# The second layer's output products with the weights held still and turned afterwards, new durations in the planner, and an earlier due time for attention

## The chip, the cores and the metric

The kernel runs on one core of a Trainium2 chip. The metric is the device time of one execution in microseconds, as the median of several runs. The profile is of one such execution.

## The reference

Three stages, one after the other. The first is a linear attention with a decay per head, in chunks of time; its output is laid out as 3072 tokens of 256 features. Two dense layers follow, each with 2048 hidden units, the first with an ELU between its products and the second with a Mish.

```python
# attention, per chunk of 32 steps (batch 4, 8 heads, 768 steps, head_dim 32, d_state 16)
cum = np.cumsum(log_a, axis=-1)
L = np.exp(cum[:, :, :, None] - cum[:, :, None, :]) * causal
y = np.einsum('bhij,bhjd->bhid', (C @ B^T) * L, x) + np.einsum('bhin,bhnd->bhid', C, state) * np.exp(cum)
state = np.exp(sum(la)) * state + sum_j B_j x_j exp(cum_last - cum_j)

x = y.transpose(0, 2, 1, 3).reshape(3072, 256)
h = x @ w_in                     # first layer
x = np.where(h > 0, h, np.exp(np.minimum(h, 0)) - 1) @ w_out
h = x @ w_in2                    # second layer
out = (h * np.tanh(np.log1p(np.exp(h)))) @ w_out2
```

## The kernel before, in words

**Tiles and blocks.** Attention goes in 32 tiles of 96 steps, eight in time for each of the four batches. The two layers go in seven blocks of tokens, BL = 384, 384, 512, 512, 512, 512, 256. The list `order` alternates layers: (1,0), (1,1), (2,0), (2,1), (1,2), (1,3), (2,2), (1,4), (2,3), and so on to (2,6), where (2,3) is layer 2 of block 3. Each block has 16 slots, one for each 128 hidden units. A slot has an h part (`emit_h`, six products: two halves of the contraction by high x high, high x low and low x high parts of the split 32-bit numbers), then the activation and the split of its result into gh and gl, and an output part some five slots later (`LAG`).

**Output products.** In layer 1 (`emit_y1`) the weights are stationary and the tokens move: two accumulators of 128 features x all tokens of the block, three products each, so six of 512 columns in a large block. In layer 2 (`emit_y2`) the activations are stationary, 128 tokens at a time, and the weights move: for each 128 tokens one product of gh with high and low weights (512 columns) and one of gl with the high weights (256 columns). The accumulator holds 128 tokens x 512 values; ScalarE or VectorE scales its second half (`y2_out1`), VectorE adds the first (`y2_out2`), and one or two DMAs store rows of 256 numbers (`y2_store`).

**PSUM.** Eight banks: two for h (`ph`), two "acc", two "accb" (`pa`), two "s" (`px`) for attention. Layer 2 takes its first two accumulators from acc and the third and fourth from accb. Layer 1 takes two from acc, and its odd slots of h from f = 5 on (or from the start, if the block before is also layer 1) from accb; this is `h_other`.

**What sets the order.** Nothing is scheduled at run time. The program lists steps, each with the engines that can do it, a duration, the steps that it needs, and sometimes a due time `dl`. `run_steps` plays these through, always takes the step whose latest start (`late`, found backwards from due times) is earliest, and writes the instructions in that order on each engine's queue. Rings (`take`) stand for buffers. `alt` gives a step to one of two engines. The due time of an h slot is `slot_time`; attention steps inherit theirs through what they feed. `lock` holds the steps of VectorE that are kept apart from GpSimd's. Loads of ScalarE's function tables ("exp", "mish") are counted in.

**Attention, as far as it is touched.** For each tile: `three_parts` (splits of B and C on ScalarE and VectorE or GpSimd, then a DMA that transposes, stk to t), `at_diff` and `at_mask` and `at_exp` (the decays d), `at_scores` (TensorE, s), `at_p` (VectorE, r), `at_y` and `at_st` (TensorE, ys), and `at_y_hi` and `at_y_lo` (the split of the output into xyh and xyl, the first layer's input). The first eight tiles go without the DMA (`at_tr0`, `at_scores0`). All loads and all stores but one are issued on SP's queue, in order.

**Weights.** Each of 32 pieces (`jobs`: i1, o1, i2, o2) is loaded as raw bits and split by `job_1` to `job_5`; `job_4` writes the high part and `job_5` the low part.

Of the kernel before, what the change touches and what calls it, by code (L numbers as in the profile page):

```python
# [18 lines left out]
def tile_chain(  # L19
# [25 lines left out]
    FP = 2  # L45
    NP = NF // FP
# [59 lines left out]
    class Need:  # L106
# [10 lines left out]
        d=Ring(2), r=Ring(1), t=Ring(1), r1=Ring(1), bw=Ring(2), o=Ring(2), stk=Ring(1),  # L117
# [264 lines left out]
    def job_4(j, eng):  # L382
        key, k = jobs[j]
        z, n = divmod(j, NJ)
        wt[key, k] = wpool.tile([128, 2, 2, 256], F32R, tag=f"w{z + 1}_{n}", name=f"w{key}{k}")
        copy(eng, w_hi(key, k), raw[j][:, :, :, 1].bitcast(F32))

    def job_5(j, eng):
        key, k = jobs[j]
        w = raw.pop(j)[:, :, :, 1].bitcast(F32)  # L390
        alu(eng).tensor_tensor(out=w_lo(key, k), in0=w, in1=w_hi(key, k).bitcast(F32), op=ALU.subtract)
# [480 lines left out]

    def emit_y2(s, k):
        _, c, f = at_slot(s)
        n = min(128, BL[c] - 128 * k)
        if f == 0:

            acc[2, c, k] = pa.tile([128, 2, DM], F32, tag="acc" if k < 2 else "accb", name="acc")[0:n]
# [4 lines left out]
        nc.tensor.matmul(out=y, lhsT=gh[:, ts], rhs=w[:, :, f % FP, :], start=(f == 0), stop=False)  # L883
        nc.tensor.matmul(out=y[:, 0], lhsT=gl[:, ts], rhs=w[:, 0, f % FP, :], start=False, stop=(f == NF - 1))  # L884

    def y2_out1(c, k, eng):
        n = min(128, BL[c] - 128 * k)
        o = tl["o", c, k] = at.tile([128, DM], F32, tag="o", name="o", bufs=2)[0:n]
        if eng == V:
            nc.vector.tensor_scalar_mul(o, acc[2, c, k][:, 1], 1.0 / WS)  # L890
        else:
            nc.scalar.activation(out=o, in_=acc[2, c, k][:, 1], func=AF.Copy, scale=1.0 / WS)
# [62 lines left out]
    s_d6 = step((PE, 0.1, decays_6), s_d5, s_c2, an)  # L955
# [8 lines left out]
    for j, (key, k) in enumerate(jobs):  # L964
# [21 lines left out]
        rf.append(q5)  # L986
        w_ready[key, k] = [q4, q5]
# [21 lines left out]
    def out_of_y(i, y):  # L1009

        YHI[i], YLO[i] = {}, {}
        for q in pieces(i):
            w = q[3] / T
            YHI[i][q[0]] = step((A, 0.14 + 0.14 * w, lambda q=q: at_y_hi(i, *q)), y, xy_f["x", q[0]][1])
            YLO[i][q[0]] = step((V, 0.10 + 0.2 * w, lambda q=q: at_y_lo(i, *q)), YHI[i][q[0]])
        return list(YHI[i].values()) + list(YLO[i].values())

    def three_parts(i, need):
# [3 lines left out]
        a1 = step((A, 0.88, lambda: at_split_1(i)), need, sn)  # L1022
        a2 = step(alt(lambda e: at_split_2(i, e), (V, 0.50), (G, 0.50)), a1, rn)
        a3 = step((A, 0.68, lambda: at_split_3(i)), a2)
        a4 = step(alt(lambda e: at_split_4(i, e), (V, 0.50), (G, 0.50)), a3)
# [17 lines left out]
    for i in range(NB):  # L1043
        cold = i in TR0
        if cold:
            tf, tn = take("s")
            tr = step((PE, 0.64, lambda i=i: at_tr0(i)), s_lc[i], s_lb[i], s_c2, tn)
# [16 lines left out]
        else:  # L1064
# [50 lines left out]
    for i in range(NB, tiles):  # L1115
# [16 lines left out]
        for g in range(2):  # L1132
            f = lambda e, i=i, g=g: at_diff(i, g * H // 2, (g + 1) * H // 2, e)
            dd.append(step(alt(f, (G, 1.0), (V, 0.47)), lc, s_q6))
            lock.add(dd[-1])
        mk = step((G, 0.95, lambda i=i: at_mask(i)), dd)
        ex = step((A, 0.78, lambda i=i: at_exp(i)), mk)
        table[ex] = "exp"
        cs = step((G, 0.95, lambda i=i: at_cs(i)), l96, lc, s_d5)
        r_f, r_n = take("r")  # L1140
        rc = step((V, 0.56, lambda i=i: at_rc(i)), cs, r_n)
# [8 lines left out]
        if cold:  # L1150
            pz = []
            for z in range(2):
                two = [take("s"), take("s")]
                sc = step((PE, 0.65, lambda i=i, z=z: at_scores0(i, z)), a2, [n for _, n in two])
# [8 lines left out]
        if c + 1 < NCH:  # L1163
            y = step((PE, 0.65, lambda i=i: (at_y(i), at_st(i))), pz, rc, rc2, LX[i], pn, SO[i - NB], b1, b2)
# [11 lines left out]
    for s in range(len(order) * NF):  # L1176
# [3 lines left out]
        if f == 0 and s:  # L1180
            acc_f[blk] = [take("acc" if k < 2 else "accb") for k in range(2 if layer == 1 else NK[c])]
# [43 lines left out]
        if layer == 1:  # L1225
# [5 lines left out]
            if f == NF - 1:  # L1231
                EV[1, c] = []
                for k in range(2):
# [3 lines left out]
                    acc_f[blk][k][0].extend([p, q])  # L1237
        else:
# [45 lines left out]
```

## Time and profile before

| | us |
|---|---|
| median of 3 runs | 613.85 (613.49 to 615.1) |
| the profiled execution | 614.17 |
| its span, first to last instruction | 612.1 |
| around the span | 2.07 |
| TensorE busy | 598.7 (98% of the span) |
| VectorE busy | 433.2 (71%) |
| ScalarE busy | 377.4 (62%) |
| GpSimd busy | 177.6 (29%) |

In the profile the engines are PE (TensorE's products), PEld (its loads of weights), DVE (VectorE), ACT (ScalarE), POOL (GpSimd) and SP (the queue of DMAs). A row of a timeline has the start in us, the duration, engine, line of the kernel, instruction, what it writes and reads, and its shape. Products overlap, so the pace of a stream is the distance between starts, not the duration of one. In brackets stands how long the engine had been idle, and what ended that. A row of the view of stretches has, for each engine, busy us and in brackets the count of instructions.

### The profile page before, as it was taken

The numbers are of one execution on the slowest core, as the hardware profiler recorded it, in microseconds if no ns is written. First come the engines' busy times: TensorE is split into PE (matmuls) and PEld (weight loads), VectorE is DVE, ScalarE is ACT, GpSimd is POOL, SyncE is SP. The second block draws the span as 40 slices with busy tenths as digits, with TensorE's granted clock in tenths as the row PEclk, the third lists the DMA queues.
The fourth block names the chain that finished last, engine by engine and source line by source line (L and its number), as shares of the span: only waits on it lengthen the run. The fifth ranks groups of instructions, "written<-read, shape, count | busy, mean of one in ns | idle before, by whom it ended". The sixth has DMA issues, their size and how long they took to land.

```text
span 612.1 us, 10993 instructions
## 1 busy us (share of the span) xinstructions
PE 598.7 (98%) x3876; PEld 506.4 (83%) x3876; DVE 433.2 (71%) x948; ACT 377.4 (62%) x705; POOL 177.6 (29%) x238
## 2 busy tenths in 40 slices
PE   6899999999999999999999999999999999999997
PEld 5677799999987878888878888878888888988896
DVE  5899899987887888765877766767764545744454
ACT  4699999976878775554786644597544214542121
POOL 2346455222556545100544301536100000200000
PEclk9599999999999999999999999999999999999999
DMA  7799894205564543002463302533300000000010
GB/s 149 190 244 297 260 260 103 56 9 99 104 121 85 111 81 68 5 0 52 72 114 73 80 1 27 104 82 74 62 0 1 1 0 19 19 1 0 1 36 18
DMA packets 133655, 47.09 MB, mean 77 GB/s; under 512 B 116672, under 2 KB 122432, under 8 KB 133600
## 3 DMA queue, kind: packets, MB, share of 16 engines
q1 hardware_dynamic: 133488, 46.29, 34.5%
q8 instruction: 30, 0.49, 0.4%
q14 instruction: 25, 0.20, 0.1%
q10 hardware_dynamic: 112, 0.10, 0.0%
HBM read 32.31 MB, written 3.24 MB: 58 GB/s over the span
## 4 chain that ended last, share of the span: by engine, by line
PE 92%; DMA 3%; ACT 2%; DVE 1%; issue 1%; SPq 0%; ACTq 0%; DVEq 0%
PE h L789 15%; PE h L790 14%; PE h L791 14%; PE acc L883 14%; PE acc L884 7%; PE acc L852 6%; PE acc L853 6%; PE acc L854 6%; PE acc L857 4%; PE ys L716 2%; DMA t<-stk 2%; PE s L667 2%; PE s L679 1%; ACT L836 1%; PE ys L746 1%
## 5 line engine op out<-in xcount | busy, mean ns | idle before, releaser
L789 PE MATMUL h<-xyh,wi 128*128 128x512 f32 (+2 forms) x448 | 168.5, 376 | 1.0 <-ACT w L836 0.9
L790 PE MATMUL h<-xyl,wi 128*128 128x512 f32 (+2 forms) x448 | 162.2, 362 | 0.2 <-DVE xyl L733 0.2
L791 PE MATMUL h<-xyh,wi 128*128 128x512 f32 (+2 forms) x448 | 162.0, 362 | 0.0
L883 PE MATMUL acc<-wo,gh 128*128 128x512 f32 x384 | 142.5, 402 | 0.0
L832 DVE TENSOR_TENSOR gl<-w,gh 128x512 fp32r<-128x512 f32 (+2 forms) x181 | 122.5, 678 | 21.5 <-ACT gh L375 12.9
L836 ACT ACTIVATE w<-h 128x512 f32<-128x512 f32 (+2 forms) x112 | 59.4, 536 | 100.9 <-PE h L791 68.7
L884 PE MATMUL acc<-wo,gl 128*128 128x256 f32 x384 | 107.5, 280 | 0.0
L377 DVE CAST gh<-w 128x512 fp32r<-128x512 f32 (+2 forms) x114 | 47.0, 414 | 74.8 <-PE acc L883 51.2
L789 PEld LDWEIGHTS h<-xyh,wi 128*128 128x128 f32 x448 | 85.0, 190 | 17.4 <-ACT w L836 2.5
L791 PEld LDWEIGHTS h<-xyh,wi 128*128 128x128 f32 x448 | 85.0, 190 | 10.7
L790 PEld LDWEIGHTS h<-xyl,wi 128*128 128x128 f32 x448 | 85.2, 190 | 9.7 <-DVE xyl L733 0.5
L883 PEld LDWEIGHTS acc<-wo,gh 128*128 128x128 f32 x384 | 72.2, 188 | 15.5
L805 ACT ACTIVATE w<-h 128x512 f32<-128x512 f32 (+2 forms) x96 | 51.7, 540 | 51.1 <-PE h L791 37.1
L884 PEld LDWEIGHTS acc<-wo,gl 128*128 128x128 f32 x384 | 72.5, 189 | 2.2
L832 POOL TENSOR_TENSOR gl<-w,gh 128x512 fp32r<-128x512 f32 (+2 forms) x27 | 29.6, 1096 | 147.6 <-ACT gh L375 95.6
L375 ACT ACTIVATE gh<-w 128x512 fp32r<-128x512 f32 (+2 forms) x94 | 54.9, 584 | 27.8 <-PE acc L853 23.4
L852 PE MATMUL acc<-gh,wo 128*128 128x512 f32 (+2 forms) x192 | 70.2, 365 | 0.0
L854 PE MATMUL acc<-gl,wo 128*128 128x512 f32 (+2 forms) x192 | 69.6, 363 | 0.0
L853 PE MATMUL acc<-gh,wo 128*128 128x512 f32 (+2 forms) x192 | 69.6, 362 | 0.0
L813 DVE TENSOR_SCALAR w<-w 128x512 f32<-128x512 f32 (+2 forms) x74 | 30.5, 414 | 26.2 <-ACT w L805 25.2
L595 POOL TENSOR_TENSOR d<-bc,dk 32x384 f32<-32x384 f32 x28 | 27.9, 999 | 68.8 <-DVE gl L832 41.8
L821 DVE TENSOR_TENSOR w<-h,w 128x512 f32<-128x512 f32 (+2 forms) x74 | 46.6, 631 | 1.5
(102 smaller groups left out, 821.4 us busy)
## 6 DMA issues: line engine op xcount, KB each, us to landing
d<-cum_d SPq DMA_DIRECT2D x31, 288.0 KB, 3.9
raw<-in_moe_w_in_dram SPq DMA_DIRECT2D x16, 512.0 KB, 6.5
raw<-in_moe_w_out_dram SPq DMA_DIRECT2D x16, 512.0 KB, 5.9
xs<-in_x_dram SPq DMA_DIRECT2D x32, 96.0 KB, 2.9
bc<-in_C_dram SPq DMA_DIRECT2D x32, 48.0 KB, 2.4
bc<-in_B_dram SPq DMA_DIRECT2D x32, 48.0 KB, 2.7
out_dram<-o SPq DMA_DIRECT2D x15, 96.0 KB, 1.9
bc<-bc SPq DMA_DIRECT2D x84, 16.0 KB, 2.4
```

Of the source, the lines that this page charges most:

```text
L375: nc.scalar.activation(out=out, in_=in_, func=AF.Copy)
L789: nc.tensor.matmul(out=h, lhsT=hi[:, k, fs], rhs=xh[:, k, :], start=(k == 0), stop=False)
L790: nc.tensor.matmul(out=h, lhsT=hi[:, k, fs], rhs=xl[:, k, :], start=False, stop=False)
L791: nc.tensor.matmul(out=h, lhsT=lo[:, k, fs], rhs=xh[:, k, :], start=False, stop=(k == 1))
L805: nc.scalar.activation(out=new_w(s), in_=st[s][0], func=AF.Exp)
L832: alu(eng).tensor_tensor(out=gl, in0=w, in1=gh.bitcast(F32), op=ALU.subtract)
L836: nc.scalar.activation(out=new_w(s), in_=st[s][0], func=AF.Mish)
L852: nc.tensor.matmul(out=y, lhsT=hi[:, f % FP, ds], rhs=gh, start=(f == 0), stop=False)
L853: nc.tensor.matmul(out=y, lhsT=lo[:, f % FP, ds], rhs=gh, start=False, stop=False)
L854: nc.tensor.matmul(out=y, lhsT=hi[:, f % FP, ds], rhs=gl, start=False, stop=(f == NF - 1))
L883: nc.tensor.matmul(out=y, lhsT=gh[:, ts], rhs=w[:, :, f % FP, :], start=(f == 0), stop=False)
L884: nc.tensor.matmul(out=y[:, 0], lhsT=gl[:, ts], rhs=w[:, 0, f % FP, :], start=False, stop=(f == NF - 1))
```

## The change

- **Output products of layer 2** in blocks 0 to 5 (`emit_yt`): as in layer 1, the weights are stationary, and there are two accumulators of 128 x tokens, from acc. At the end of a block VectorE turns each accumulator in squares of 32 x 32 into SBUF (`yt_turn`), ScalarE or VectorE scales the whole in place (`yt_scale`), and one DMA for each 32 tokens stores it (`yt_store`), in pieces of 64 numbers. Block 6 keeps `emit_y2`, with its views changed to the new order of columns; its last addition is split in two.
- **Weights o2** are written by `job_4` and `job_5` with columns regrouped, so that the turned squares land in order (`by_rows`, `from_raw`).
- **Banks**: no accumulator takes accb any more. `h_other` puts every odd slot of h there, in both layers, but for block 6 of layer 2 and the first slots.
- **Planner**: durations of attention's steps are changed, most for TensorE and GpSimd.
- **Due time**: the split `at_y_lo` of tiles from 14 on gets one, 10 us (`EARLY`) before the first slot that reads it.

The diff, cut to its core:

```diff
+    EARLY = 10.0
...
+    def by_rows(key, w):
+        return w.rearrange("p k f (b q) -> p (f b) k q", q=32) if key == "o2" else w
+
+    def from_raw(key, r):
+        w = r[:, :, :, 1].bitcast(F32)
+        return w.rearrange("p f (b k q) -> p (f b) k q", k=2, q=32) if key == "o2" else w
...
-        copy(eng, w_hi(key, k), raw[j][:, :, :, 1].bitcast(F32))
+        copy(eng, by_rows(key, w_hi(key, k)), from_raw(key, raw[j]))
...
-        return layer == 1 and f % 2 and (f >= 5 or s >= NF and order[s // NF - 1][0] == 1)
+        return f % 2 and (f >= 5 or s >= NF and (c < NBL - 1 or layer == 1))
...
+    def emit_yt(s):
+
+        _, c, f = at_slot(s)
+        if f == 0:
+            acc[2, c] = [pa.tile([128, MT], F32, tag="acc", name="acc")[:, 0:BL[c]] for _ in range(2)]
+        _, _, gh, gl = st.pop(s)
+        hi, lo = [w("o2", f // FP)[:, :, f % FP] for w in (w_hi, w_lo)]
+        for k in range(2):
+            y = acc[2, c][k]
+            nc.tensor.matmul(out=y, lhsT=hi[:, k], rhs=gh, start=(f == 0), stop=False)
+            nc.tensor.matmul(out=y, lhsT=lo[:, k], rhs=gh, start=False, stop=False)
+            nc.tensor.matmul(out=y, lhsT=hi[:, k], rhs=gl, start=False, stop=(f == NF - 1))
+
+    def yt_turn(c, k):
+        if k == 0:
+            tl["t", c] = at.tile([128, MT // 32, 64], F32, tag="raw", name="turned")
+        nc.vector.transpose(
+            out=tl["t", c][:, 0:BL[c] // 32, 32 * k:32 * k + 32],
+            in_=acc[2, c][k].rearrange("p (g t) -> p g t", t=32),
+        )
+
+    def yt_scale(c, eng):
+        t = tl["t", c][:, 0:BL[c] // 32]
+        if eng == A:
+            nc.scalar.activation(out=t, in_=t, func=AF.Copy, scale=1.0 / WS)
+        else:
+            nc.vector.tensor_scalar_mul(t, t, 1.0 / WS)
+
+    def yt_store(c, p):
+        tile_, i = divmod(BS[c] + p, T)
+        n = min(T - i, BL[c] - p)
+        r0 = (tile_ % NB) * S + (tile_ // NB) * T + i
+        for g in range(n // 32):
+            r = r0 + 32 * g
+            nc.sync.dma_start(
+                out=out[r:r + 32, :].rearrange("t (b e) -> b t e", b=4), in_=tl["t", c][:, p // 32 + g]
+            )
...
     def y2_out2(c, k):
-        o = tl["o", c, k]
-        nc.vector.scalar_tensor_tensor(
-            out=o, in0=acc[2, c, k][:, 0], scalar=1.0 / WS, in1=o, op0=ALU.mult, op1=ALU.add
-        )
+        a, b = in_rows(acc[2, c, k][:, 0], tl["o", c, k])
+        for j in range(2):
+            nc.vector.scalar_tensor_tensor(
+                out=b[:, j], in0=a[:, j], scalar=1.0 / WS, in1=b[:, j], op0=ALU.mult, op1=ALU.add
+            )
...
-        s_d4 = step((PE, 0.15, lambda t=t: decays_4(t)), s_d1, an)
+        s_d4 = step((PE, 0.77, lambda t=t: decays_4(t)), s_d1, an)
...
-            YLO[i][q[0]] = step((V, 0.10 + 0.2 * w, lambda q=q: at_y_lo(i, *q)), YHI[i][q[0]])
+            dl = slot_time(order.index((1, q[0])) * NF) - EARLY if i >= 14 else 1e9
+            YLO[i][q[0]] = step((V, 0.10 + 0.2 * w, lambda q=q: at_y_lo(i, *q)), YHI[i][q[0]], dl=dl)
...
-        a2 = step(alt(lambda e: at_split_2(i, e), (V, 0.50), (G, 0.50)), a1, rn)
+        a2 = step(alt(lambda e: at_split_2(i, e), (V, 0.46), (G, 0.82)), a1, rn)
...
-            sc = step((PE, 0.4 if cold else 0.38, lambda z=z: at_scores(i, z)), a5, pn)
+            sc = step((PE, 0.19, lambda z=z: at_scores(i, z)), a5, pn)
...
-            acc_f[blk] = [take("acc" if k < 2 else "accb") for k in range(2 if layer == 1 else NK[c])]
+            acc_f[blk] = [take("acc") for _ in range(2)]
...
+        elif c < NBL - 1:
+            y = YS[s] = step((PE, pe, lambda s=s: emit_yt(s)), ydep, an, YS.get(s - 1, []), dl=ydl)
+            gf.append(y)
+            lf.append(y)
+            if f == NF - 1:
+                tf, tn = take("turned")
+                if c == 0:
+                    tn = raw_f
+                turned = []
+                for k in range(2):
+                    turned.append(step((V, ct, lambda c=c, k=k: yt_turn(c, k)), y, tn))
+                    acc_f[blk][k][0].append(turned[-1])
+                o = step(alt(lambda e, c=c: yt_scale(c, e), (A, 0.12 + n * 0.0016), (V, 0.09 + n * 0.00116)), turned)
+                lock.add(o)
```

**Where the order moves.** Three places. The names are the program's tiles with buffer numbers.

TensorE, one slot of layer 2 in a block of 512, before: six h products, then four pairs into four accumulators.

```order
L789 MATMUL h_6612<-xyh_5775,wi24_1504 128x512
L790 MATMUL h_6612<-xyl_5776,wi24_1504 128x512
L791 MATMUL h_6612<-xyh_5775,wi24_1504 128x512
L883 MATMUL acc_6544<-wo22_1568,gh_6577 128x512
L884 MATMUL acc_6544<-wo22_1568,gl_6579 128x256
L883 MATMUL acc_6547<-wo22_1568,gh_6577 128x512
L884 MATMUL acc_6547<-wo22_1568,gl_6579 128x256
L883 MATMUL acc_6550<-wo22_1568,gh_6577 128x512
L884 MATMUL acc_6550<-wo22_1568,gl_6579 128x256
L883 MATMUL acc_6553<-wo22_1568,gh_6577 128x512
L884 MATMUL acc_6553<-wo22_1568,gl_6579 128x256
```

The same with the change: three products into each of two accumulators.

```order
L799 MATMUL h_6595<-xyh_5702,wi27_1728 128x512
L800 MATMUL h_6595<-xyl_5703,wi27_1728 128x512
L801 MATMUL h_6595<-xyh_5702,wi27_1728 128x512
L892 MATMUL acc_6442<-gh_6564,wo24_1681 128x512
L893 MATMUL acc_6442<-gh_6564,wo24_1681 128x512
L894 MATMUL acc_6442<-gl_6566,wo24_1681 128x512
L892 MATMUL acc_6443<-gh_6564,wo24_1681 128x512
L893 MATMUL acc_6443<-gh_6564,wo24_1681 128x512
L894 MATMUL acc_6443<-gl_6566,wo24_1681 128x512
```

The slot has 12 products instead of 14, all of 512 columns, and the weights (wo) are now what is held still.

VectorE at the end of block 3 of layer 2, before: the additions of four accumulators between the first layer's activations (w, h) and splits (gl).

```order
L896 SCALAR_TENSOR_TENSOR o_5392<-acc_4804,o_5392 128x256
L813 TENSOR_SCALAR w_5406<-w_5406 128x512
L821 TENSOR_TENSOR w_5406<-h_5384,w_5406 128x512
L813 TENSOR_SCALAR w_5412<-w_5412 128x512
L896 SCALAR_TENSOR_TENSOR o_5418<-acc_4809,o_5418 128x256
L821 TENSOR_TENSOR w_5412<-h_5397,w_5412 128x512
L896 SCALAR_TENSOR_TENSOR o_5435<-acc_4827,o_5435 128x256
L685 TENSOR_TENSOR r_5293<-s_5421,d_5149 96x384
L685 TENSOR_TENSOR r_5293<-s_5429,d_5149 96x384
L832 TENSOR_TENSOR gl_5463<-w_5406,gh_5461 128x512
L896 SCALAR_TENSOR_TENSOR o_5474<-acc_4838,o_5474 128x256
```

The same with the change.

```order
L823 TENSOR_SCALAR w_5343<-w_5343 128x512
L899 STREAM_TRANSPOSE turned_5355<-acc_4888 128x16x32
L899 STREAM_TRANSPOSE turned_5355<-acc_4889 128x16x32
L831 TENSOR_TENSOR w_5343<-h_5325,w_5343 128x512
L823 TENSOR_SCALAR w_5369<-w_5369 128x512
L831 TENSOR_TENSOR w_5369<-h_5346,w_5369 128x512
L842 TENSOR_TENSOR gl_5395<-w_5322,gh_5390 128x512
```

Two turns stand together where four additions stood apart; attention's step (r) is no longer there at this point.

GpSimd in the first 25 us, before: four masks (d) follow the products bw.

```order
L576 TENSOR_TENSOR bw_164<-bc0_113,dk_93 96x128
L576 TENSOR_TENSOR bw_170<-bc0_113,dk_93 96x128
L566 AFFINE_SELECT d_168<-d_168 96x768
L566 AFFINE_SELECT d_143<-d_143 96x768
L566 AFFINE_SELECT d_152<-d_152 96x768
L566 AFFINE_SELECT d_185<-d_185 96x768
```

The same with the change.

```order
L586 TENSOR_TENSOR bw_149<-bc0_113,dk_93 96x128
L586 TENSOR_TENSOR bw_155<-bc0_113,dk_93 96x128
L572 TENSOR_TENSOR d_147<-d_147,dk_93 96x384
L576 AFFINE_SELECT d_182<-d_182 96x768
L576 AFFINE_SELECT d_147<-d_147 96x768
L576 AFFINE_SELECT d_157<-d_157 96x768
L572 TENSOR_TENSOR d_174<-d_174,dk_93 96x384 x2
L576 AFFINE_SELECT d_174<-d_174 96x768
```

Three of the additions (d from d and dk) that stood on VectorE have come between the masks.

## Rows read from the trace of the kernel before

**Rows 1.** The page's busy times, and TensorE's granted clock in 40 slices of 15.3 us

```profile
PE 598.7 (98%) x3876; PEld 506.4 (83%) x3876; DVE 433.2 (71%) x948; ACT 377.4 (62%) x705; POOL 177.6 (29%) x238
...
PEclk9599999999999999999999999999999999999999
```

**Rows 2.** Waits of TensorE (PE) and of its weight loads (PEld): total, times, longest, in us

```profile
PE p_cr L646 <- DVE cum L448: 4.3, 1, 4.3
...
PE h L789 <- ACT w L836: 0.9, 3, 0.5
...
PEld h L789 <- ACT w L836: 2.5, 6, 0.8
...
PEld L679 <- DMA t<-stk: 1.2, 2, 0.7
```

**Rows 3.** Timeline of TensorE, first layer, blocks of 512: start, duration, instruction

```profile
461.11 0.39 PE L789 MATMUL h<-xyh,wi 128*128 128x512 f32 x1
...
462.47 0.39 PE L852 MATMUL acc<-gh,wo 128*128 128x512 f32 x1
...
469.27 0.39 PE L789 MATMUL h<-xyh,wi 128*128 128x512 f32 x1
```

**Rows 4.** Timeline of TensorE, second layer, block of 512

```profile
555.23 0.40 PE L789 MATMUL h<-xyh,wi 128*128 128x512 f32 x1
...
560.79 0.40 PE L789 MATMUL h<-xyh,wi 128*128 128x512 f32 x1
...
562.17 0.39 PE L883 MATMUL acc<-wo,gh 128*128 128x512 f32 x1
...
563.57 0.40 PE L789 MATMUL h<-xyh,wi 128*128 128x512 f32 x1
...
571.93 0.40 PE L789 MATMUL h<-xyh,wi 128*128 128x512 f32 x1
```

**Rows 5.** Timeline of TensorE, blocks of 384: first layer, then second

```profile
89.53 0.33 PE L789 MATMUL h<-xyh,wi 128*128 128x384 f32 x1
...
97.85 0.33 PE L789 MATMUL h<-xyh,wi 128*128 128x384 f32 x1
...
126.96 0.34 PE L789 MATMUL h<-xyh,wi 128*128 128x384 f32 x1
...
135.28 0.34 PE L789 MATMUL h<-xyh,wi 128*128 128x384 f32 x1
```

**Rows 6.** Groups by line and shape: busy us, mean ns | idle before, releasers

```profile
L617 DVE STREAM_TRANSPOSE r<-d 32x384 f32<-32x384 f32 x28 | 16.0, 573 | 1.8 <-POOL d L595 0.8 <-PE ys L716 0.4
...
L868 DVE SCALAR_TENSOR_TENSOR xyl<-acc,xyh 128x512 fp32r<-128x512 f32 x8 | 5.1, 682 | 0.0
...
L896 DVE SCALAR_TENSOR_TENSOR o<-acc,o 128x256 f32<-128x256 f32 x24 | 9.8, 420 | 3.8 <-ACT o L892 3.6
...
L836 ACT ACT_TABLE_LOAD x18 | 23.1, 1283 | 2.7 <-DVE gl L832 2.4
...
L562 DVE TENSOR_TENSOR d<-d,dk 96x384 f32<-96x384 f32 x30 | 17.6, 607 | 2.5 <-DMA d<-cum_d 2.3
...
L375 ACT ACTIVATE wo<-raw 128x512 fp32r<-128x512 f32 x13 | 8.6, 671 | 0.1
```

**Rows 7.** Start: busy us (count) of PE, PEld, DVE, ACT, POOL; clock, DMA share, GB/s

```profile
14.30:24.40 10.10, 8.36 (x119) 6.07 (x118) 8.60 (x27) 7.25 (x15) 2.16 (x3) 0.50 0.85 241
...
24.40:31.50 7.10, 7.04 (x40) 6.13 (x41) 5.93 (x17) 4.53 (x9) 3.83 (x4) 0.50 0.61 133
```

**Rows 8.** The same view for a later stretch

```profile
150.00:200.00 50.00, 49.20 (x386) 42.20 (x385) 41.15 (x101) 41.44 (x78) 27.87 (x38) 1.00 0.58 107
```

**Rows 9.** Timeline of all engines at the end

```profile
607.29 0.73 ACT L892 ACTIVATE o<-acc 128x256 f32<-128x256 f32 x2 [2.64 <-PE acc L884]
...
607.70 0.77 DVE L896 SCALAR_TENSOR_TENSOR o<-acc,o 128x256 f32<-128x256 f32 x2 [1.33 <-ACT o L892]
...
608.15 1.75 SPq L909 DMA_DIRECT2D out_dram<-o  x3
```

More of the change, by code (lines that the diff above doesn't have):

```diff
@@ L116, in tile_chain @@
         w=Ring(WB), gh=Ring(GB), gl=Ring(GB), h=Ring(HB), acc=Ring(2), accb=Ring(2), s=Ring(2), xy=Ring(3), x=Ring(5), bc=Ring(2),
-        d=Ring(2), r=Ring(1), t=Ring(1), r1=Ring(1), bw=Ring(2), o=Ring(2), stk=Ring(1),
+        d=Ring(2), r=Ring(1), t=Ring(1), r1=Ring(1), bw=Ring(2), o=Ring(2), stk=Ring(1), turned=Ring(1),
     )
@@ L384, in job_4 @@
         z, n = divmod(j, NJ)
-        wt[key, k] = wpool.tile([128, 2, 2, 256], F32R, tag=f"w{z + 1}_{n}", name=f"w{key}{k}")
-        copy(eng, w_hi(key, k), raw[j][:, :, :, 1].bitcast(F32))
+        shape = [128, 2, 2, FP, 128] if key == "o2" else [128, 2, 2, 256]
+        wt[key, k] = wpool.tile(shape, F32R, tag=f"w{z + 1}_{n}", name=f"w{key}{k}")
+        copy(eng, by_rows(key, w_hi(key, k)), from_raw(key, raw[j]))
     def job_5(j, eng):
         key, k = jobs[j]
-        w = raw.pop(j)[:, :, :, 1].bitcast(F32)
-        alu(eng).tensor_tensor(out=w_lo(key, k), in0=w, in1=w_hi(key, k).bitcast(F32), op=ALU.subtract)
+        hi, lo = by_rows(key, w_hi(key, k)), by_rows(key, w_lo(key, k))
+        alu(eng).tensor_tensor(out=lo, in0=from_raw(key, raw.pop(j)), in1=hi.bitcast(F32), op=ALU.subtract)
     nc.scalar.preload_act_table_set("natural_log_exp_and_others")
@@ L876, in emit_y2 @@
         if f == 0:
-            acc[2, c, k] = pa.tile([128, 2, DM], F32, tag="acc" if k < 2 else "accb", name="acc")[0:n]
+            acc[2, c, k] = pa.tile([128, 2, DM], F32, tag="acc", name="acc")[0:n]
         _, _, gh, gl = st[s]
@@ L882, in emit_y2, with in_rows @@
         ts = slice(k * 128, k * 128 + n)
-        nc.tensor.matmul(out=y, lhsT=gh[:, ts], rhs=w[:, :, f % FP, :], start=(f == 0), stop=False)
-        nc.tensor.matmul(out=y[:, 0], lhsT=gl[:, ts], rhs=w[:, 0, f % FP, :], start=False, stop=(f == NF - 1))
+        yk = y.rearrange("p z (k e) -> p z k e", k=2)
+        nc.tensor.matmul(out=yk, lhsT=gh[:, ts], rhs=w[:, :, :, f % FP, :], start=(f == 0), stop=False)
+        nc.tensor.matmul(
+            out=yk[:, 0], lhsT=gl[:, ts], rhs=w[:, 0, :, f % FP, :], start=False, stop=(f == NF - 1)
+        )
+    def in_rows(y, o):
+        return y.rearrange("p (k b q) -> p k b q", k=2, b=4), o.rearrange("p (b k q) -> p k b q", k=2, b=4)
     def y2_out1(c, k, eng):
@@ L888, in y2_out1 @@
         o = tl["o", c, k] = at.tile([128, DM], F32, tag="o", name="o", bufs=2)[0:n]
+        a, b = in_rows(acc[2, c, k][:, 1], o)
         if eng == V:
[L890 removed]
+            nc.vector.tensor_scalar_mul(b, a, 1.0 / WS)
         else:
[L892 removed]
+            nc.scalar.activation(out=b, in_=a, func=AF.Copy, scale=1.0 / WS)
     def y2_out2(c, k):
[L895 to L898 removed]
+        a, b = in_rows(acc[2, c, k][:, 0], tl["o", c, k])
+        for j in range(2):
+            nc.vector.scalar_tensor_tensor(
+                out=b[:, j], in0=a[:, j], scalar=1.0 / WS, in1=b[:, j], op0=ALU.mult, op1=ALU.add
+            )
     def y2_store(c, k):
@@ L1153, in tile_chain @@
                 two = [take("s"), take("s")]
-                sc = step((PE, 0.65, lambda i=i, z=z: at_scores0(i, z)), a2, [n for _, n in two])
+                sc = step((PE, 0.55, lambda i=i, z=z: at_scores0(i, z)), a2, [n for _, n in two])
                 tf.append(sc)
@@ L1237, in tile_chain @@
                     acc_f[blk][k][0].extend([p, q])
+        elif c < NBL - 1:
[12 more added lines that the diff above has]
+                lock.add(o)
+                p = 0
+                while p < n:
+                    m = min(T - (BS[c] + p) % T, n - p)
+                    tf.append(step((DQ, 0.5 * (m // 32), lambda c=c, p=p: yt_store(c, p), 0.3), o))
+                    p += m
         else:
```

29 lines of the change are left out of this document (15 added, 14 removed).

## The prediction

> **What bounds the kernel now.** I read the busy times and the clock line first. TensorE is busy for 598.7 of 612.1 us, and its clock is granted in full from the third slice on [rows 1]. A busy TensorE need not be one at its best pace, so I looked next at who keeps it waiting. The one long wait is the first, 4.3 us before the first product. Later, what it loses is small: products of the first layer's type (h) wait for ScalarE to free a PSUM bank, and scores wait for a transposing DMA [rows 2]. So from the first product of the blocks to the last one, the time is the length of TensorE's stream, and the question is how long one slot of that stream takes. A slot is one slice of 128 hidden units: six h products, and the output products of a slice five slots earlier.
>
> In the first layer a slot with 512 tokens takes (469.27 - 461.11) / 3 = 2.72 us, and its h half 462.47 - 461.11 = 1.36 us, so 0.227 us for a product of 512 columns [rows 3]. In the second layer it takes (571.93 - 555.23) / 6 = 2.783 us: 562.17 - 560.79 = 1.38 us for the same six h products and 563.57 - 562.17 = 1.40 us for the four pairs of 512 and 256 columns [rows 4]. Both slots stream 6144 columns. With 384 tokens, both layers take 2.08 us, (97.85 - 89.53) / 4 and (135.28 - 126.96) / 4 [rows 5].
>
> **The output products (the main term).** In six of the second layer's seven blocks the pairs become six products like the first layer's. For 512 tokens that is the same mix as in the first layer: twelve products of 512 columns with 128 weights each. I take its 2.72 us. The four blocks of 512 have 64 slots: 64 x 0.063 = 4.05 us less. The reason I expect the h products to recover as well: they have the same shape and operands in both layers, and what stands between them in the second layer is a run that alternates 512 and 256 columns. The bound below: if the h half stays at 1.38 us and the output half comes down to it, the slot is 2.76 us and the gain 64 x 0.023 = 1.5 us. In the two blocks of 384 nothing is gained, and the last block keeps its pairs.
>
> A rule of the Trainium skill speaks against this term. "TensorE: Matmul & The Clock Gate", section "Back-to-back issue gap", puts the isolated gap between products at the columns over 2.4 GHz and a small constant of 2.5 ns. By that, equal columns are equal time and only two constants go per slot: an estimate of 64 x 5 ns = 0.3 us instead of 4.05. The rows show a longer pace than this rule, and two different ones for equal columns, so I go by the rows.
>
> **What frees the accumulators.** Before, four of them (two in the ring "acc", two in "accb") were scaled and added by ScalarE and VectorE. Now there are two, and each is turned by one VectorE instruction; until both are done the next block cannot begin its output products. The trace has a turn of 384 columns on 32 partitions, 573 ns; another VectorE instruction that reads PSUM at 512 columns takes 682 ns [rows 6]. I take 0.7 us. The first accumulator is complete three products, 0.68 us, before the second, so both are free about 2 x 0.7 - 0.68 = 0.7 us after the last product, and some 0.4 us more for two handovers: 1.1 us. Between the last output product of a block and the first of the next, TensorE's order has two h slices, 2 x 1.36 = 2.72 us (2.08 with 384 tokens). Behind the turns on VectorE stand the splits of the next slices; with three buffers of each half they are not due at once. I cost the turns at nothing. Upper bound: if the four groups of 32 partitions were served one after another, a turn would take four times 573 ns at 384 columns, 3.06 us at 512. The point at which it decides is 2T - 0.68 + 0.4 = 2.72, T = 1.5 us.
>
> **The banks of h and the order of attention.** Since accb is no longer an accumulator, odd slices of h in the second layer use it: four banks instead of two. That is aimed at the wait that TensorE's weight loads show most, 2.5 us for ScalarE; the earlier due time of attention is aimed at the 1.2 us for the DMA [rows 2]. Both could go: -3.7 us. Against it, the new order loads ScalarE's tables 44 times instead of 36, at 1.283 us each [rows 6], 10 us more on an engine that is busy 41.4 of 50 us in a stretch in which it serves attention beside the second layer [rows 8]. If a third of that reached TensorE it would be +3.4 us. I take -1.0 us, nearer to the gain, because two more banks let TensorE run on while ScalarE is late, and because ScalarE also gives up 20 of its 22 copies of the outputs, 0.37 us each [rows 9], for five scalings.
>
> **The start.** From 14.3 to 24.4 us TensorE idles 1.74 us and VectorE is busy 8.60 of 10.10 us [rows 7]: VectorE sets the pace there. Before the first block's input is complete, three of its additions go to GpSimd and two copies come to it. At most 0.607 us each [rows 6], that is 1.8 off and 1.2 on: -0.6 us. Bounds: all of the idle time gained or as much lost, -1.74 to +1.74. The granted clock is 0.50 in this stretch and the next [rows 7]; the 7.0 us of work from 24.4 us on would take half at full clock, so a full clock that comes 3 us earlier or later is worth 1.5 us either way. I take no change of it and leave it to the range.
>
> **Covered or small.** The stores: 88 of 32 rows instead of 44 larger ones on SP's queue, 0.58 us each by the three that take 1.75 us [rows 9]. The longest run is 16, 9.3 us, with a transposing DMA for scores queued behind it; TensorE's order has eight slots, over 20 us, before those scores. Cost nothing; without that cover, up to 9 us once. The weights of the second layer's output are copied in another order of columns: same count; if each of the copies (671 ns [rows 6]) took half as long again, that is 8 x 0.34 us on an engine with 8.6 us to spare [rows 8]. Nothing. At the end, the last addition of 256 columns (420 ns [rows 6]) becomes two of 128: between nothing and another 0.42 us, since each has a fixed part; I take +0.15 us. It has no cover, the store waits for it [rows 9].
>
> **The sum.** The profiled execution took 614.17 us, 612.1 of span and 2.07 around it. 614.17 - 4.05 - 1.0 - 0.6 + 0.15 = 608.7. That execution is 0.32 us above the median of the three runs shown, so the forecast for the median is 608.4 us.
>
> **The rivals.**
> - *Columns alone count.* The slower pace belongs to the second layer and not to its products of 256 columns. For it: h products with equal operands are slower there too, 0.230 against 0.227 us. Against it: blocks of 384, which also alternate, lose nothing. Only 1.5 us are gained: 614.17 - 1.5 - 1.0 - 0.6 + 0.15 - 0.32 = 610.9. By the Trainium skill's constant ("TensorE: Matmul & The Clock Gate", "Back-to-back issue gap") an estimate in the same way is 612.1.
> - *ScalarE becomes the bound around attention.* The table loads reach TensorE (+3.4) and half of the start's idle time is lost again (+0.9): 614.17 - 4.05 + 3.4 + 0.9 + 0.15 - 0.32 = 614.3. For it: a ScalarE that is already four fifths busy and on the chain. Against it: the banks. No change that can be told.
> - *The turn is slow* (ends slower). At 3.06 us a turn, each of four ends of blocks of 512 is late by 2 x 3.06 - 0.68 + 0.4 - 2.72 = 3.1 us and each of two of 384 by 2 x 2.29 - 0.52 + 0.4 - 2.08 = 2.4 us, 17 in all: 608.4 + 17 = 625. Against it: the turn of 32 partitions in the trace takes hardly more than an ordinary instruction, as if each partition had a lane of its own.
>
> **How the numbers follow.** Forecast 0.72, columns alone 0.14, ScalarE 0.10, slow turn 0.04. The range goes down to 605.4, where the waits and the start's idle time are mostly gained, and up to 612.0, which takes in the first rival; the other two and the tails are left out. A measurement of this kernel tells about 0.3% from no change, 1.8 us. Faster: 0.72 + 0.12 of the first rival + 0.02 of the second = 0.86. Slower: the slow turn and a bad end of ScalarE's, 0.05. The rest, 0.09, is the same.
>
> **What would show it.** Right: a slot of the second layer at 2.72 us with 512 tokens, six products 0.227 us apart in both halves; turns near 0.7 us; no wait of the first output product of a block. Wrong: h products still 0.230 us apart; output products that wait for a turn; h products that wait longer than 2.5 us in all for ScalarE; a first h product later than before.

## The result, and the profile after

The changed kernel takes **607.19 us** (607.0 to 607.63, 4 runs) against 614.28 us of the kernel before on the same chip (613.49 to 615.1): a ratio of 0.9886, 95% interval 0.9868 to 0.9903, so 1.1% faster. In a later series, beside other kernels, it took 608.22 us (607.03 to 611.34, 6 runs) against 614.07, ratio 0.9912 (0.9892 to 0.9932). The forecast was 608.4 us in a range of 605.4 to 612.0. In two of the runs below one execution each took far longer (1150.5 and 1177.9 us), and it is left out of the median.

The profiled execution took 607.63 us, 605.6 of span. Its page, against [rows 1]:

```profile
PE 592.8 (98%) x3748; PEld 501.8 (83%) x3748; DVE 432.1 (71%) x939; ACT 391.0 (65%) x714; POOL 165.0 (27%) x222
...
PEclk9599999999999999999999999999999999999999
```

TensorE issues 128 products fewer (3748, was 3876) and is busy 5.9 us less. ScalarE is busy 13.6 us more, and that costs nothing, as will be seen. Next the waits, answering [rows 2] (total, times, longest, in us):

```profile
PE p_cr L656 <- DVE cum L458: 4.4, 1, 4.4
PE s L677 <- DVE r L683: 1.9, 1, 1.9
PE ys L756 <- DVE xs L766: 1.1, 2, 0.9
PE ys L726 <- DVE r L683: 0.7, 1, 0.7
PE h L799 <- DVE g L829: 0.2, 1, 0.2
```

That is the whole list of TensorE. The wait of h for ScalarE is gone, that of the scores for the transposing DMA too (0.5 us of weight loads are left, none of products), and no output product waits for a turn. What is left stands before 33 us, at the start.

TensorE's timeline in the second layer, a block of 512, answers [rows 4]:

```profile
549.60 0.39 PE L799 MATMUL h<-xyh,wi 128*128 128x512 f32 x1
...
550.96 0.39 PE L892 MATMUL acc<-gh,wo 128*128 128x512 f32 x1
...
552.32 0.39 PE L799 MATMUL h<-xyh,wi 128*128 128x512 f32 x1
...
555.04 0.39 PE L799 MATMUL h<-xyh,wi 128*128 128x512 f32 x1
```

The slot is 2.72 us (was 2.783), its halves 1.36 and 1.36 (were 1.38 and 1.40): the first layer's pace of [rows 3]. With 384 tokens nothing moved, against [rows 5]: six h products and six output products take 1.04 us each, 2.08 together:

```profile
152.35 0.34 PE L799 MATMUL h<-xyh,wi 128*128 128x384 f32 x1
...
153.39 0.34 PE L799 MATMUL h<-xyh,wi 128*128 128x384 f32 x1
...
154.43 0.34 PE L892 MATMUL acc<-gh,wo 128*128 128x384 f32 x1
...
155.47 0.34 PE L892 MATMUL acc<-gh,wo 128*128 128x384 f32 x1
```

The groups of the turn and of the table loads before Mish (busy us, mean ns; compare [rows 6]):

```profile
L899 DVE STREAM_TRANSPOSE turned<-acc 128x512 f32<-128x512 f32 x8 | 5.4, 705 | 1.6 <-PE acc L894 1.6
...
L846 ACT ACT_TABLE_LOAD x22 | 28.2, 1283 | 2.7 <-DVE gl L842 2.3
```

And the two stretches of the start and the later one (columns as in [rows 7, 8]):

```profile
14.30:24.40 10.10, 8.68 (x128) 6.55 (x128) 9.00 (x26) 7.70 (x16) 4.32 (x5) 0.59 0.82 224
24.40:31.50 7.10, 6.19 (x37) 5.22 (x38) 6.29 (x17) 5.65 (x13) 4.51 (x7) 0.62 0.87 198
...
150.00:200.00 50.00, 50.00 (x394) 45.24 (x394) 40.98 (x102) 44.59 (x81) 24.56 (x35) 1.00 0.56 104
```

From 150 to 200 us ScalarE is busy 44.59 us (was 41.44), and TensorE loses nothing at all: 50.00 of 50 (was 49.20).

One measure is used below, because it repeats well: the time from the first h product of the second block (at 69 us) to the last product. Before it was 538.14 us; in the two profiled executions of the changed kernel it was 531.63 and 531.50, so 6.5 us less. I call it the time behind the start.

### The profile page after: what moved, and what is told of

The parts are those of the page before. It is cut to its first block, busy times and chain, and to the rows that moved or that the text cites. A ratio compares the mean times of both kernels' runs of the same rounds, so it can differ in the third digit from the quotient of the medians.

```text
span 605.6 us, 10727 instructions
## 1 busy us (share of the span) xinstructions
PE 592.8 (98%) x3748; PEld 501.8 (83%) x3748; DVE 432.1 (71%) x939; ACT 391.0 (65%) x714; POOL 165.0 (27%) x222
## 4 chain that ended last, share of the span: by engine, by line
PE 96%; DVE 2%; ACT 0%; DMA 0%; issue 0%; POOL 0%; DVEq 0%; POOLq 0%
PE h L799 15%; PE h L801 15%; PE h L800 14%; PE acc L892 7%; PE acc L894 7%; PE acc L893 7%; PE acc L862 7%; PE acc L864 6%; PE acc L863 6%; PE acc L867 3%; PE ys L726 3%; PE s L689 1%; PE acc L932 1%; PE s L677 1%; PE acc L933 1%; PE ys L756 1%
## 5 line engine op out<-in xcount | busy, mean ns | idle before, releaser
L386 DVE CAST gh<-w 128x512 fp32r<-128x512 f32 (+2 forms) x102 | 41.2, 404 | 70.3 <-PE acc L893 43.5
L842 POOL TENSOR_TENSOR gl<-w,gh 128x384 fp32r<-128x384 f32 (+2 forms) x22 | 23.8, 1080 | 237.7 <-ACT gh L384 161.3
L384 ACT ACTIVATE gh<-w 128x512 fp32r<-128x512 f32 (+2 forms) x106 | 60.1, 568 | 37.6 <-PE acc L863 23.9
L892 PE MATMUL acc<-gh,wo 128*128 128x512 f32 (+1 forms) x192 | 73.3, 382 | 0.0
L894 PE MATMUL acc<-gl,wo 128*128 128x512 f32 (+1 forms) x192 | 71.5, 372 | 0.0
L893 PE MATMUL acc<-gh,wo 128*128 128x512 f32 (+1 forms) x192 | 71.4, 372 | 0.0
L572 POOL TENSOR_TENSOR d<-d,dk 96x384 f32<-96x384 f32 x42 | 35.4, 852 | 43.2 <-DVE stk L559 7.4
L831 DVE TENSOR_TENSOR w<-h,w 128x512 f32<-128x512 f32 (+2 forms) x68 | 41.5, 611 | 1.5
L862 PEld LDWEIGHTS acc<-gh,wo 128*128 128x128 f32 x192 | 36.2, 189 | 5.1
```

The costliest lines, as they stand in the source:

```text
L384: nc.scalar.activation(out=out, in_=in_, func=AF.Copy)
L842: alu(eng).tensor_tensor(out=gl, in0=w, in1=gh.bitcast(F32), op=ALU.subtract)
L862: nc.tensor.matmul(out=y, lhsT=hi[:, f % FP, ds], rhs=gh, start=(f == 0), stop=False)
L892: nc.tensor.matmul(out=y, lhsT=hi[:, k], rhs=gh, start=(f == 0), stop=False)
L893: nc.tensor.matmul(out=y, lhsT=lo[:, k], rhs=gh, start=False, stop=False)
L894: nc.tensor.matmul(out=y, lhsT=hi[:, k], rhs=gl, start=False, stop=(f == NF - 1))
```

## Experiments on the output products: is it the mixture of sizes?

My theory was that 256-column products among those of 512 slow the stream, their own part and the h products behind them. The rival was that equal columns cost equal time, and that the pace goes with something else of the second layer.

**512 and 256 again, with the weights still stationary.** In the blocks of 512, in each of the two accumulators, the second product is cut:

```diff
             nc.tensor.matmul(out=y, lhsT=hi[:, k], rhs=gh, start=(f == 0), stop=False)
-            nc.tensor.matmul(out=y, lhsT=lo[:, k], rhs=gh, start=False, stop=False)
+            nc.tensor.matmul(out=y[:, 0:256], lhsT=lo[:, k], rhs=gh[:, 0:256], start=False, stop=False)
             nc.tensor.matmul(out=y, lhsT=hi[:, k], rhs=gl, start=False, stop=...)
+            nc.tensor.matmul(out=y[:, 256:], lhsT=lo[:, k], rhs=gh[:, 256:], start=False, stop=...)
```

> The changed kernel; in the four blocks of 512 tokens alone the third and sixth of eight output products come as 512, 256, 512, 256 columns again, the blocks of 384 stay as in the change. Theory (by the records of the run with 512 and 256 in all blocks, where the blocks of 512 took 3.1 us more and the 192-column products of the other two the rest): 3.1 us above the change, 610.3 us; undisturbed slot 2.78 us. Rival (that run was slow for its 192-column products alone): 607.2 us.

Measured: 611.04 us (610.28 to 615.92), 2.8 above the changed kernel in the same series. Behind the start it took 3.4 us more, 0.2 of them one wait for the transposing DMA. TensorE's timeline:

```profile
555.63 0.40 PE L799 MATMUL h<-xyh,wi 128*128 128x512 f32 x1
...
557.02 0.39 PE L897 MATMUL acc<-gh,wo 128*128 128x512 f32 x1
...
558.42 0.40 PE L799 MATMUL h<-xyh,wi 128*128 128x512 f32 x1
...
561.21 0.40 PE L799 MATMUL h<-xyh,wi 128*128 128x512 f32 x1
```

The slot is back at (561.21 - 555.63) / 2 = 2.79 us, with halves of 1.39 and 1.40: within a hundredth the kernel before, though operands, banks, turns and order are those of the change. So in the blocks of 512 the sizes make the pace, and columns alone do not count.

**The same products in another order**: 512, 256, 256, 512. The last two lines above change places.

> The same products as in the run that alternates 512 and 256 in the blocks of 512 tokens, in another order: 512, 256, 256, 512, twice a slice, so half as many changes of size. Theory one (what costs is that there are 256-column products, each with its fixed part, and the pace is lost after them however they stand): as the alternating run, 610.3 us, slot 2.78 us, h half 1.38 us. Theory two (each change from one size to another costs): only the fixed part of two more products, 0.025 us a slot, and half of the remaining 0.038: 64 x 0.044 x 3.1 / 4.0 = 2.2 us above the change, 609.4 us, slot 2.764 us.

Measured: 610.13 us (609.4 to 613.47), 1.9 above the change. The timeline:

```profile
557.88 0.39 PE L799 MATMUL h<-xyh,wi 128*128 128x512 f32 x1
...
559.24 0.39 PE L897 MATMUL acc<-gh,wo 128*128 128x512 f32 x1
...
560.63 0.39 PE L799 MATMUL h<-xyh,wi 128*128 128x512 f32 x1
```

The slot is 2.75 us and its h half 1.36, as fast as in the change. The output half is 1.39: two more products a slot, and one of 256 columns comes 0.120 us before the next, one of 512 0.227, so 2 x (2 x 0.120 - 0.227) = 0.026 us. What is left over of the alternating order's loss, the slower h products above all, goes away when the two small products stand side by side. Neither theory had the size: the first expected 2.78 us, the second 2.764. Whether the changes of size count, or that a small product stood last before h, is not separated by this run, but by the next.

**All blocks mixed, and all products small.** The first cuts the second product in every block, so the blocks of 384 have 192-column products; the other cuts all six at half the block's columns (m), but for the first slot of a block:

```diff
+            for lhs, rhs in ((hi, gh), (lo, gh), (hi, gl)):
+                for ts in [slice(0, BL[c])] if f == 0 else [slice(0, m), slice(m, BL[c])]:
+                    nc.tensor.matmul(out=y[:, ts], lhsT=lhs[:, k], rhs=rhs[:, ts], ...)
```

> The changed kernel, but in each slice two of the six output products are cut in two: the run of sizes is 512, 256, 512, 256 and so on, as in the kernel before, with the output weights still stationary, the same banks, turns and order. Theory (the mixture of sizes costs): a 512-token slot goes back to the 2.78 us of before, the output half to about 1.40 and the h half to 1.37 to 1.38; 64 slots x 0.05 to 0.063 us = 3.3 to 4.0 us slower than the change, 610.5 to 611.2 us. Rival (the pace belongs to which operand is stationary, to the banks or to the place in the program): slot unchanged at 2.72 us, 607.2 us.

> The changed kernel, but all output products of six blocks (but for the first slice of a block, where one or more stays whole) are cut in halves: 12 products of 256 (or 192) columns instead of 6 of 512 (or 384). Theory (each product has a fixed part: two of 256 take 2 x 0.1197, one of 512 takes 0.2267, so 0.0127 us for each product more): 6 x 0.0127 = 0.076 us a slot, in 96 slots 7.3 us slower than the change, 614.5 us; the h products stay at 0.227 since nothing alternates within the run. Rival one (h products are slowed too whenever sizes mix): another 0.02 us x 96, 616.4 us. Rival two (columns alone count): 607.2 us.

Measured: 614.54 us (613.68 to 618.02, 11 runs) and 621.02 us (620.92 to 621.11): 7.4 and 13.8 above the change's 607.19, twice what I expected. In the records the blocks of 512 took 3.1 and 4.8 us more. For the first that is near the 3.3 of the theory. For the second it is near 64 x 0.076 = 4.9, but by luck, for the h products did not stay at 0.227 us. Its timeline in a block of 512:

```profile
562.08 0.40 PE L799 MATMUL h<-xyh,wi 128*128 128x512 f32 x1
...
563.46 0.64 PE L895 MATMUL acc<-gh,wo 128*128 128x256 f32 x4
...
564.90 0.40 PE L799 MATMUL h<-xyh,wi 128*128 128x512 f32 x1
```

The slot is 2.82 us, the output half 1.44 (twelve products of 0.120), and the h half 1.38 to 1.39, as slow as in the alternating order. So rival one was right about the h products. It also settles what the order 512, 256, 256, 512 left open: here the size changes only twice a slot, there four times, and yet h is slow here and not there. In the blocks of 512, the h products are slow in every order in which a small product stands last before them (also in the run with 512 and 256 in all blocks), and not in the two in which a large one does (the change's, and 512, 256, 256, 512).

The rest of both losses came mostly from a case that I had not costed, the products of 192 columns in the blocks of 384 (2.8 and 8.6 us in the records). In the first, 1.0 us more was lost in the first block, in which none of the cut products stand. The timeline of the kernel with all products cut, in a block of 384:

```profile
120.92 0.61 PE L895 MATMUL acc<-gh,wo 128*128 128x192 f32 x4
121.37 0.38 PE L895 MATMUL acc<-gl,wo 128*128 128x192 f32 x2
121.59 0.61 PE L895 MATMUL acc<-gh,wo 128*128 128x192 f32 x4
```

Six take 121.59 - 120.92 = 0.67 us, 0.112 each, hardly less than one of 256 (0.120) and far more than half of one of 384 (0.174). The Trainium skill, "TensorE: Matmul & The Clock Gate", section "LDWEIGHTS (loading the stationary operand)", counts the columns of the weights over 1.2 GHz, for 128 an estimate of 107 ns. The 112 ns lie near it; that the load of weights sets them is not shown. It is no least distance after every product: in the run with 384 and 192 mixed, the product behind one of 192 columns began 0.088 us after it.

## Experiments on the planner, the banks and the due time

**Products, turns and banks alone**: the change with all of the planner's old durations, and no due time.

```diff
-        s_d4 = step((PE, 0.77, lambda t=t: decays_4(t)), s_d1, an)
+        s_d4 = step((PE, 0.15, lambda t=t: decays_4(t)), s_d1, an)
...
-            YLO[i][q[0]] = step((V, 0.10 + 0.2 * w, lambda q=q: at_y_lo(i, *q)), YHI[i][q[0]], dl=dl)
+            YLO[i][q[0]] = step((V, 0.10 + 0.2 * w, lambda q=q: at_y_lo(i, *q)), YHI[i][q[0]])
```

> The changed kernel with the planner's old durations and without the due time: only the products, turns and banks of the change. Theory (pace -3.3 us; the four banks remove the waits for ScalarE, some 1.6 us of the gaps of before at 178.7, 183.6, 187.3 and 398.9 us, while the scores still wait for the DMA): 614.3 - 3.3 - 1.6 = 609.4 us. Rival (the waits go by the planner's order, not by banks): 614.3 - 3.3 = 611.0 us. Rival two (the products alone give everything): 607.2 us.

Measured: 610.27 us (609.51 to 610.48), 3.9 less than before. Its waits:

```profile
PE s L688 <- DMA t<-stk: 1.5, 1, 1.5
...
PE ys L725 <- DVE r L694: 0.7, 1, 0.7
```

No h waits for ScalarE here, though the planner is the old one; the scores and the attention behind them still come late, by more than before. Behind the start it took 534.23 us, 3.9 less than before.

**The planner's part alone**: the new durations and the due time on the old products and banks (the reverse of that diff, in the kernel before).

> The kernel before with the planner's new durations and the due time alone; products, accumulators and banks as before. Theory (it takes away the scores' waits for the DMA, 0.9 us in the gaps at 318.7 and 414.8 us, and little else): 613.4 us. Rival (the order takes away all the gaps, 3.1 us): 611.2 us. Rival two (without the banks the 8 more table loads on ScalarE reach TensorE): 615 us or more.

Measured: 613.02 us (612.2 to 614.52, 10 runs), ratio 0.9979 (0.9968 to 0.9991): 1.2 us faster, near what the theory had. The scores' waits are gone, as it said, but other waits have come:

```profile
PE acc L885 <- DVE gl L833: 1.5, 1, 1.5
...
PE h L790 <- ACT w L837: 1.0, 1, 1.0
```

I read this so: with attention earlier, ScalarE and VectorE are late for the layers, and two banks cannot bridge that. Alone the halves give 3.9 and 1.2 us by the medians; together they gave 7.1 in the first series and 5.9 in the later one. Behind the start they give 3.9 and 0.7 alone and 6.5 together, in both profiled executions.

**The change without its four banks of h.**

```diff
-        return f % 2 and (f >= 5 or s >= NF and (c < NBL - 1 or layer == 1))
+        return layer == 1 and f % 2 and (f >= 5 or s >= NF and order[s // NF - 1][0] == 1)
```

> The changed kernel, but h of the second layer keeps to the banks it had before. Theory (the four banks carry the waits for ScalarE): the planner's part on the old products showed one such wait of 1.1 us and one of 1.7 us for a split; here they come back, 608.3 to 610.0 us. Rival (once the copies of the outputs are gone from ScalarE and VectorE, two banks are enough): 607.2 us.

Measured: 611.16 us (609.62 to 612.71), above the expected 608.3 to 610.0. In its records the last product is 2.4 us later than in the change, 0.4 of it already at the first h product; behind the start it took 2.0 us more. Three waits are new:

```profile
PE s L689 <- DMA t<-stk: 0.9, 1, 0.9
...
PE acc L894 <- DVE gl L842: 0.4, 1, 0.4
...
PE h L799 <- ACT w L846: 0.2, 1, 0.2
```

So two banks are not enough even when the copies of the outputs are off ScalarE, and the banks are worth some 2 us. The waits that I expected (1.1 us for ScalarE, 1.7 for a split) came back only in small part, 0.2 and 0.4 us. The banks also shift the planner's order: the longest of these waits is one for the DMA.

**The change without the due time**, the new durations kept.

> The changed kernel without attention's own due time; the planner's new durations stay. Theory (the due time is what brings the transposing DMA early enough for the scores): waits as in the kernel with the old durations and no due time come back, 1.6 us at 174 and 0.9 us at 320: 609.7 us. Rival (the durations alone order attention early enough): 607.2 us.

Measured: 611.32 us (610.14 to 611.55); the last product is 2.8 us later, 2.7 behind the start. The size was near the expected 2.5, the place was another. It is not the scores that wait, but the first h product of block 3, at 234 us, for its own input:

```profile
PE h L798 <- ACT xyh L737: 2.0, 1, 2.0
...
PE ys L725 <- DVE r L694: 0.5, 1, 0.5
```

The due time is set on the second half of just this input (`at_y_lo`). Behind the start this kernel took 534.31 us, and the one with the old durations and no due time 534.23. So the new durations by themselves gave nothing there, and the planner's share came with the due time. The due time with the old durations was not run.

## Experiments on the turns

Each turn done twice, and four times:

```diff
+        for _ in range(2):
             nc.vector.transpose(out=tl["t", c][...], in_=acc[2, c][k].rearrange(...))
```

> The changed kernel with each of the twelve turns done twice, so T = 1.4 us with 512 tokens and 1.1 with 384; order and planner's costs unchanged. The prediction's step (T decides from 1.5 us on): no change, 607.2 us. Rival (slack as the trace of the change shows it, from the end of the second turn to the first product of the next block: 0.43, 2.0, 1.8, 1.6, 0.9 and 0.5 us at the six ends): 1.1 - 0.43 + 1.4 - 0.9 + 1.4 - 0.5 = 2.1 us, 609.3 us.

> The changed kernel with each turn done four times, T = 2.8 us with 512 tokens, near the slow turn of 3.06 us of the prediction's rival. The prediction's formula: 2 x 2.8 - 0.68 + 0.4 - 2.72 = 2.6 us at four ends and 2 x 2.14 - 0.52 + 0.4 - 2.08 = 2.1 us at two, 14.6 us in all, 621.8 us. By the slack in the trace of the change: 3.2 - 0.43, 3.2 - 2.0, 4.2 - 1.8, 4.2 - 1.6, 4.2 - 0.9, 4.2 - 0.5 us, 16.0 in all, 623.2 us. Rival (TensorE runs ahead enough, only VectorE's load counts): 607.2 us.

Measured: 610.43 us (610.14 to 611.82) and 628.58 us (627.55 to 630.32). With two, the waits are

```profile
PE s L689 <- DMA t<-stk: 1.3, 1, 1.3
...
PE acc L892 <- DVE turned L900: 0.3, 1, 0.3
PE acc L862 <- DVE turned L900: 0.3, 1, 0.3
```

Two of the six ends of a block wait for the turn. One is that of a block of 512, at T = 1.4 us, while my formula put the deciding point at 1.5. The other is that of a block of 384, at T = 1.1 us, which is where the same formula puts it (2T - 0.52 + 0.4 = 2.08). More is lost where I didn't look: VectorE is later with the attention behind it, and a transposing DMA lands 1.3 us late. With four:

```profile
PE acc L862 <- DVE turned L900: 8.5, 6, 2.3
...
PE acc L933 <- DVE turned L900: 2.6, 2, 1.6
PE acc L892 <- DVE turned L900: 2.5, 2, 1.6
PE s L689 <- DMA t<-stk: 1.4, 1, 1.4
```

The turns cost 13.6 us of waiting, near the 14.6 of the formula, but the last product is 22.7 us late. The windows of this kernel (columns as in [rows 7]) show where a part of the rest is:

```profile
200.00:203.50 3.50, 1.82 (x7) 0.89 (x6) 3.36 (x7) 0.60 (x1) 3.38 (x5) 1.00 0.95 179
203.50:207.20 3.70, 3.70 (x10) 2.89 (x11) 2.84 (x8) 2.19 (x5) 0.00 (x0) 0.56 0.03 7
...
446.30:449.50 3.20, 3.20 (x9) 2.44 (x9) 2.65 (x5) 1.87 (x4) 0.00 (x0) 0.50 0.15 33
...
535.00:538.40 3.40, 3.40 (x17) 3.40 (x17) 2.46 (x7) 1.87 (x4) 0.00 (x0) 0.50 0.12 26
```

Behind three of the waits (1.38 us up to 203.50, 1.91 up to 445.10 and 2.26 up to 534.93) the granted clock falls from 2.4 to 1.2 GHz (0.50 of full): 3.70 x 0.44 + 3.20 x 0.50 + 3.40 x 0.50 = 4.9 us of work lost. With the 1.4 us for the DMA that makes 19.9 of the 22.7; the remaining 2.8 I did not place.

## Why the prediction was right, point by point

In the records of the two profiled executions the last product starts 6.40 us earlier (600.92, was 607.32), and the first h product 0.09 later (25.80, was 25.71). So all of the gain lies between them, and all of it behind the start: 6.5 us there, as told above.

- **Output products**: mechanism right, size too large. I took 64 x 0.063 = 4.05 us. Putting the old sizes back in the blocks of 512 cost 3.1 us in the records when all blocks were mixed; when these alone were, it cost 2.8 us by the medians and 3.2 in the records without the wait for the DMA: 0.044 to 0.050 us a slot. The 0.063 was read from the one undisturbed stretch, and I applied it to all 64 slots. In the run with all blocks mixed, the blocks 2 to 5 cost 0.84, 0.80, 0.60 and 0.86 us more than in the change, where 16 x 0.063 would be 1.0 each: pieces of attention stand between the products of the first three, and the last outputs of blocks 4 and 5 run beside h products of 256 columns. The nothing for blocks of 384 was right.
- **The rule of the Trainium skill** ("TensorE: Matmul & The Clock Gate", "Back-to-back issue gap") would have given 0.3 us, an estimate from a constant that the page states for a product by itself. The measurement decides against it: 3 us.
- **Columns alone count** (the first rival) fell with the alternating run.
- **Banks and order of attention**: right in sign, too small. I took -1.0 within -3.7 to +3.4; 6.5 less 3.1 to 3.2 leaves about 3.3 us, near the bound on the good side. That the banks count is shown: without them 2.0 us are lost. My reason for them, that TensorE runs on while ScalarE is late, holds only in part: without the banks 0.2 us of wait were for ScalarE and 0.9 for the DMA. The due time is worth 2.7 us, but at the first layer's input and not at the scores, where I aimed it. The two overlap with each other and with the products, for 3.2, 2.0 and 2.7 are more than the 6.5 in all.
- **ScalarE becomes the bound** (the second rival): the eight more table loads are there (44), and ScalarE is as full as feared, but nothing of it reached TensorE.
- **Turns at no cost**: right; 0.705 us (0.7 taken). The room was smaller than the 1.6 us that I worked out: in the trace of the change, from the end of the second turn to the next block's first output product, 0.43 us at the first end and 0.5 to 2.0 at the others, as VectorE had other work when the last product was done. So at some ends the deciding point lies lower than 1.5 us.
- **The slow turn**: a turn of 2.8 us was made, and cost 21 us, where the rival had 17 for one of 3.06; partly by the clock, which the rival left out.
- **The start**: wrong, and one of the signs that I had named. I took -0.6, and the first h product came 0.09 later (run again, 0.31 earlier). The step that failed was that VectorE's count of instructions sets the pace there: three additions left it, and still it is busy 9.00 us (was 8.60) and TensorE waits 1.9 us in one piece for it. The first h product is late although TensorE has less to do in front of it: eight products of scores stood before it and now stand behind it. The rows of before and of the change:

```profile
24.82 0.96 PE L667 MATMUL s<-f32t 16*96 16x96 f32 x8
...
31.37 0.58 PE L677 MATMUL s<-f32t 16*96 16x96 f32 x8
```

The half clock also ended earlier (0.62 granted from 24.4 to 31.5 us, was 0.50), but by the second block of the first layer the change was 0.11 us behind: these eight products and two new waits of 0.2 us each, at 32 us, took that back.

- **The tail**: +0.15 taken, and 0.1 gained: ScalarE's first scaling begins 4.76 us before the end, was 4.86 [rows 9]. The step itself held: from that scaling to the first of the last stores it is 0.97 us, was 0.86. What was gained came behind it, 0.2 us from there to the end, which I had not forecast.

```profile
600.89 0.73 ACT L947 ACTIVATE o<-acc 128x256 f32<-128x256 f32 x2 [2.64 <-PE acc L933]
...
601.30 0.89 DVE L952 SCALAR_TENSOR_TENSOR o<-acc,o 128x128 f32<-128x128 f32 x4 [1.33 <-ACT o L947]
601.86 1.78 SPq L965 DMA_DIRECT2D out_dram<-o  x3
```

So the forecast came within 1.2 us with some luck, by errors of opposite signs: 0.9 too much for the products and 0.7 for the start, against some 2.3 too little for the waits and 0.25 at the tail.

## What to carry to other kernels

Where TensorE is full, count products, not columns: cut the same work into fewer and larger ones of one size. If small ones are needed, put them side by side and a large one between them and a long run of large ones, as in 512, 256, 256, 512. Read a pace from all stretches that it will be applied to, not from the cleanest. Parts of a change that remove waits can be worth more together than alone: attention made earlier gave 0.7 us behind the start on the old products and banks, and 2.6 on the new ones.

## What the runs showed of the hardware that I had not expected

- The pace of a product depends on those before it: six equal h products take 1.36 us behind 512, 256, 256, 512 columns and 1.39 behind 512, 256, 512, 256 or behind twelve of 256. In the blocks of 384 of the kernel before, pairs of 512 and 256 slowed nothing (2.08 us a slot [rows 5]). The cause within TensorE stays open.
- In a run of small products alone, each with its own load of 128 weights, one takes 0.112 us with 192 columns and 0.120 with 256.
- A wait of 1.4 to 2.3 us amid a full stream can be followed by a stretch in which TensorE is granted 1.2 instead of 2.4 GHz, as in the three windows above. The length of the wait alone does not decide it: after 1.91 us up to 348.08 us in the same run, as long as the one before the second fall, and after 2.0 us in the run without the due time, the clock stayed full.
- The start differs among executions of nearly the same program. In the run with 512, 256, 256, 512 the clock fell a second time, and its profiled execution was 4.2 us late by 69 us, while the changed kernel run again was 1.0 us late there. The two windows of the former:

```profile
32.00:36.00 4.00, 3.51 (x27) 2.52 (x27) 2.89 (x10) 2.67 (x7) 2.42 (x5) 0.75 0.97 259
36.00:40.00 4.00, 4.00 (x18) 3.83 (x19) 2.66 (x8) 3.04 (x6) 2.18 (x4) 0.50 0.85 238
```

The changed kernel once more, for which I had written

> The changed kernel once more, beside the two others on the same chip: 607.2 us, and with another execution's records, where its start may differ by some 0.4 us as it does among the runs so far (first h product at 25.80 to 26.23 us).

had its first h product at 25.40 us and gave the 608.22 us told above, 1.0 more than expected. Its first block took 1.4 us longer than in the other profile, by a wait of 1.4 us for VectorE at 31 us; behind the start the two agree to 0.13 us. Differences of some 1 us between two single profiles are therefore not read as effects of an edit here when they arise before 69 us.
